# Five tiles in the old form and two pairs, or three tiles and three pairs

## The chip, the cores and the metric

The kernel runs on one core of one Trainium2 chip. The metric is the device time of one execution in microseconds (us); the kernel before takes 1206.51 us, the median of 3 runs (1205.77 to 1207.02). TensorE is called PE, its weight loads PEld, VectorE DVE, ScalarE ACT, GpSimd POOL and SyncE, which issues all DMAs here, SP.

## The reference

Two stages follow one another. The first is a linear attention over 8 batches of 8 heads, 576 positions of width 64, with 128 random features; the second is a gated feed-forward over the 4608 resulting rows of width 512, with a hidden width of 1536. All is float32.

```python
q_p, k_p = phi(q * scale), phi(k * scale)    # phi(x) = exp(h - max h) / sqrt(m), h = x @ omega.T - |x|^2 / 2
kv = einsum('bhsm,bhsd->bhmd', k_p, v);  z = sum(k_p, axis=2)
attn = einsum('bhsm,bhmd->bhsd', q_p, kv) / (einsum('bhsm,bhm->bhs', q_p, z) + 1e-6)
x = attn.transpose(0, 2, 1, 3).reshape(4608, 512)
g = x @ w_gate;  val = x @ w_val             # 512 x 1536 each
out = (g * sigmoid(g) * val) @ w_out         # 1536 x 512
```

## The kernel before, in words

**Attention.** Its work is cut into groups of 256 rows of a pair of heads, 72 groups of q and 72 of k, two groups to a step, so 72 steps (`steps`, `NS`). A loop over n runs the pieces of several steps side by side: transposes of the inputs (`st_transpose`, tile pt, four transposes a step), the projections on omega (`st_project`, tile pp, 16 matmuls a step), the maximum on DVE (`st_max`), eight exponentials on ACT (`st_exp`, tile ph), the sums over k (`k_accumulate`, tile kvacc), and, one to three steps later, q's part (`q_transpose`, `q_mult`, `q_norm`, `q_out`; tiles ptq, po, xt). For batches 0 to 3 `q_mult` works on PE (po), from batch 4 on the normalisation runs on POOL and DVE instead (jk, dj). `q_out` gives columns of x, transposed.

**Feed-forward, old form.** The 4608 rows are 9 tiles of 512. The hidden width is 12 pieces of 128 (f), in 4 sets of 3. A *visit* is one tile with one set: 3 x 12 matmuls for the gate (tile g), 3 x 12 for the value (tile v, both line 657), and 4 x 9 for the way down (tile o, line 666). Every float32 product is three products of a high and a low part (names ending in hi/hh/xh and lo/hl/xl), so the weights and x are split first. The visits go round by round (`ROUNDS`): for every set, all tiles of the round. Before a set's first visit the weights of the next set are fetched from a scratch in DRAM (tile wraw) and split by ACT and POOL (`load_weights`, whi and wlo).

**Feed-forward, new form.** The last tiles go in pairs (`PAIRS`). Two tiles and two pieces of the hidden width make 2 x 2 blocks; seven block products (`ORDER`, line 872, tiles a, c, d, six matmuls each) take the place of eight. `make_seven` forms the seven combinations of the weights on DVE (line 848 and the three after it), `first_x` and `next_x` form those of x on DVE (line 827 in `next_x`), `plus`, `gate` and `value` add the products up on DVE and ACT. The way down stays as it was. One pair has 12 x 42 = 504 products and 288 matmuls of the way down. `next_x` for the following pair starts in a pair's second visit: four DMAs (line 823) and eight subtractions.

**Order of the work.** The first `EARLY` = 25 steps (order `CLOSE`) hold no feed-forward. From then on (order `GROUPED`) every step has six places (`SHARE`) at which `give` takes matmuls from the generator `stream` until the amount that `course` sets for that step is reached. `course` spreads all visits but the last 45 us (`MARGIN`) evenly over the steps to the end, kept below what is available by then. That gave 5.43 us of visits in steps 25 to 33 and 9.40 us from step 34 on, in the planner's own costs. What is left after the last step, 45 us by the same costs, runs while `first_x` prepares the first pair; then the pairs follow.

**Conversion of the weights.** All 36 weight blocks are loaded raw (tiles st), turned into float32 numbers by six operations each (`convert_all`: lines 268 and 276 on ACT, 270, 272 and 274 on DVE, 278 on POOL) and written to the scratch. `tick` issues one operation; `marks` paces them so that a set is ready when its first visit is near. In the profile seven of them end in the first 128.4 us, 12 in the next 97.6 us and 17 in the 264 us after that; the last were due at step 50 (`DENSE`).

```python
for k_ in range(1, NSET):
    at = int(np.searchsorted(course, cum[len(ROUNDS[0]) * k_ - 1]))
    marks.append((max(at, marks[-1][0] + 1), 3 * FA * (k_ + 1)))
DENSE = marks[-1][0]
```

Of the kernel before, what the change touches and what calls it, by code (L numbers as in the profile page):

```python
# [23 lines left out]
def kernel(  # L24
# [34 lines left out]

    ROUNDS = [range(0, 3), range(3, 5)]
    PAIRS = [(5, 6), (7, 8)]
    NPF = NF // 2
    MARGIN = 45.0

# [99 lines left out]
    visits = []  # L166
    for r, tiles in enumerate(ROUNDS):
        sets = list(range(NSET))[:: 1 if r % 2 == 0 else -1]
# [41 lines left out]
# [3 lines that stand above are left out]
# [458 lines left out]
    acc = {}  # L671
    paired = [j for pair in PAIRS for j in pair]

# [117 lines left out]
    def first_x():  # L791

        win = late_pools["win"]
        for c in range(CH):
            x = {}
            for name, j, o in (("b11", 0, 0), ("b21", 0, CH), ("t1", 1, 0), ("b22", 1, CH), ("t3", None, None)):
                x[name] = win.tile([P, T], F32, name=f"first_{name}{c}", tag="first", bufs=5)
                if j is not None:
                    nc.sync.dma_start(x[name], x_dram[PAIRS[0][j]][:, c + o, :])
            yield  # L800
# [18 lines left out]
    def next_x(r):  # L819

        for half, names in ((0, ("b11", "t1")), (1, ("b21", "b22"))):
            for j, name in zip(PAIRS[r], names):
                nc.sync.dma_start(ahead[name], x_dram[j][:, half * CH : (half + 1) * CH, :])
        yield
        for o, a, b in (("t3", "b22", "t1"), ("t1", "t1", "b11"), ("t2", "b22", "t1"), ("t4", "b21", "t2")):
            for c in range(CH):
                nc.vector.tensor_tensor(ahead[o][:, c], ahead[a][:, c], ahead[b][:, c], op=ALU.subtract)
                yield
# [38 lines left out]
    def product(ps, n, wts, start):  # L867
# [10 lines left out]
    pair_visits = [  # L878
        (r, k_, pf) for r in range(len(PAIRS)) for k_, pf in enumerate(list(range(NPF))[:: 1 if r % 2 == 0 else -1])
    ]  # L880

    def pair_rounds(todo):
# [51 lines left out]
        for vi, (r, k_, pf) in enumerate(pair_visits):  # L934
            unit = [0]
            then = pair_visits[vi + 1] if vi + 1 < len(pair_visits) else None
            new_x = then and then[0] != r
            if k_ == 1 and r + 1 < len(PAIRS):
                prep = next_x(r + 1)
# [57 lines left out]
            wts2 = {f: weights[f, 2] for f in (2 * pf, 2 * pf + 1)}  # L997
            for j, o in ((PAIRS[r][1], 1), (PAIRS[r][0], 0)):
                ht = {2 * pf + n: h[2 * n + o] for n in range(2)}
# [124 lines left out]
```

## Time and profile before

| | |
|---|---|
| time, median of 3 runs | 1206.51 us |
| profiled execution, its own time | 1207.78 us |
| its span on the core | 1206.0 us |
| PE busy | 1165.7 us (97%) |
| ACT, DVE, POOL busy | 679.9, 595.7, 572.7 us |
| ACT table loads (exponential and Silu in turn) | 28 and 29, 1283 ns each |
| matmuls of lines 657, 666, 872 | 1440, 1104, 1008 |

A busy share is the union of an engine's instructions; the ends of matmuls are modelled, so a busy PE may still be waiting a little. Times in the views are us from the start of the span. In the tables by window each engine has its busy time and, as (x...), its instructions in the window.

### The profile page before, as it was taken

To read this page: it belongs to the slowest core of one execution; us is meant where nothing else is said; L and a number is where in the kernel's file an instruction comes from. 1 tells how busy PE (TensorE), PEld (TensorE's weight loads), DVE (VectorE), ACT (ScalarE), POOL (GpSimd) and SP (SyncE) were. 2 spreads that over 40 slices of the span, in tenths; PEclk is the share of its full clock that TensorE was granted. 3 is DMA by queue.
4 is the path that set the end of the run, shared out by engine and by line. 5 is a ranking of instruction groups with operands and counts; after the bars stand their busy time and mean duration, and the time that the engine had idled before them with its cause. 6 is when DMAs were issued, how large, how long until landed. Compare 5 with 4: busy or idle time off the path is not lost.

```text
span 1206.0 us, 18814 instructions
## 1 busy us (share of the span) xinstructions
PE 1165.7 (97%) x6705; PEld 964.4 (80%) x6705; DVE 595.7 (49%) x1159; ACT 679.9 (56%) x1497; POOL 572.7 (47%) x500
## 2 busy tenths in 40 slices
PE   6999999999999999999999999999899999999998
PEld 5888787877887778888888787878688888888886
DVE  3687674345454644434332353373534556535544
ACT  4888977576566555556465656343454435454431
POOL 3333343334254546535445776344655543555541
PEclk9999999999999999999999999999999999999999
DMA  6555665344344423345222221334311111321103
GB/s 150 141 136 142 164 201 159 87 125 134 103 118 131 138 74 79 79 107 122 62 60 68 71 66 45 106 87 139 88 53 53 53 44 27 105 53 53 53 18 70
DMA packets 174110, 113.53 MB, mean 94 GB/s; under 512 B 125856, under 2 KB 144320, under 8 KB 174016
## 3 DMA queue, kind: packets, MB, share of 16 engines
q1 hardware_dynamic: 174016, 112.32, 34.9%
q8 instruction: 53, 0.87, 0.3%
q14 instruction: 41, 0.34, 0.1%
HBM read 87.10 MB, written 25.18 MB: 93 GB/s over the span
## 4 chain that ended last, share of the span: by engine, by line
PE 66%; DMA 4%; DVE 3%; POOL 3%; ACT 3%; issue 2%; SPq 1%; POOLq 0%; ACTq 0%; DVEq 0%
PE o L666 22%; PE a L872 10%; PE v L657 8%; PE g L657 8%; PE c L872 5%; PE pp L406 3%; PE d L872 2%; PE kvacc L540 2%; PE ptq L564 2%; PE xt L621 1%; PE pt L383 1%; POOL wlo L251 1%; DMA st<-in_moe_w_out_dram 1%; ACT ph L438 1%; DMA nat<-in_k_dram 1%
## 5 line engine op out<-in xcount | busy, mean ns | idle before, releaser
L438 ACT ACTIVATE ph<-pp,st 128x128 f32<-128x128 f32 x576 | 157.6, 389 | 17.0 <-DVE st L427 16.4
L695 DVE TENSOR_TENSOR acc<-o,acc 128x512 f32<-128x512 f32 x140 | 95.7, 685 | 104.7 <-PE o L666 104.7
L390 POOL TENSOR_TENSOR sq<-nat 128x512 f32<-128x512 f32 x72 | 75.6, 1051 | 146.0 <-DMA nat<-in_k_dram 116.9
L424 DVE TENSOR_REDUCE st<-pp 128x4 f32<-128x512 f32 x144 | 92.8, 683 | 72.5 <-PE pp L406 72.3
L251 POOL TENSOR_TENSOR wlo<-wraw,whi 128x512 fp32r<-128x512 f32 x76 | 99.9, 1324 | 55.3 <-ACT whi L250 55.1
L666 PE MATMUL o<-whi,hh 128*128 128x512 f32 x240 | 97.3, 406 | 3.1 <-ACT sl L731 3.0
L666 PE MATMUL o<-whi,hl 128*128 128x512 f32 x240 | 95.1, 396 | 1.2 <-POOL hl L754 1.2
L657 PE MATMUL g<-xh,whi 128*128 128x512 f32 x240 | 96.1, 400 | 0.0
L657 PE MATMUL v<-xh,whi 128*128 128x512 f32 x240 | 95.7, 399 | 0.2 <-DVE acc L695 0.2
L500 POOL TENSOR_TENSOR jk<-ph,zt 128x512 f32<-128x512 f32 x32 | 41.6, 1305 | 112.8 <-ACT ph L438 112.8
L666 PE MATMUL o<-wlo,hh 128*128 128x512 f32 x240 | 95.1, 396 | 0.0
L406 PE MATMUL pp<-omT,x 64*128 64x128 f32 x1152 | 92.8, 297 | 2.3 <-ACT x L391 2.2
L657 PE MATMUL g<-xh,wlo 128*128 128x512 f32 x240 | 94.0, 392 | 0.0
L657 PE MATMUL v<-xh,wlo 128*128 128x512 f32 x240 | 93.8, 391 | 0.0
L657 PE MATMUL g<-xl,whi 128*128 128x512 f32 x240 | 93.8, 391 | 0.0
L657 PE MATMUL v<-xl,whi 128*128 128x512 f32 x240 | 93.6, 390 | 0.0
L754 POOL TENSOR_TENSOR hl<-sl,hh 128x512 fp32r<-128x512 f32 x60 | 79.0, 1320 | 27.1 <-ACT hh L753 26.9
L406 PEld LDWEIGHTS pp<-omT,x 64*128 64x128 f32 x1152 | 76.0, 196 | 19.1 <-issue 11.6
L417 DVE TENSOR_REDUCE st<-sq 128x8 f32<-128x512 f32 x72 | 49.1, 681 | 85.5 <-POOL sq L390 85.4
L863 POOL TENSOR_TENSOR wlo<-s,whi 128x512 fp32r<-128x512 f32 x44 | 65.3, 1502 | 34.3 <-DVE late L969 11.8
L863 POOL TENSOR_TENSOR wlo<-wraw,whi 128x256 fp32r<-128x256 f32 (+1 forms) x44 | 45.2, 1026 | 74.9 <-ACT whi L862 74.7
L540 PE MATMUL kvacc<-v,ph 128*128 128x65 f32 x512 | 69.3, 277 | 3.4 <-ACT ph L438 3.4
(251 smaller groups left out, 2854.8 us busy)
## 6 DMA issues: line engine op xcount, KB each, us to landing
wraw<-wscr SPq DMA_DIRECT2D x120, 256.0 KB, 2.7
wscr<-wc SPq DMA_DIRECT2D x36, 256.0 KB, 2.4
out_dram<-acc SPq DMA_DIRECT2D x72, 128.0 KB, 2.3
nat<-in_k_dram SPq DMA_DIRECT2D x64, 128.0 KB, 3.1
v<-in_v_dram SPq DMA_DIRECT2D x64, 128.0 KB, 3.2
nat<-in_q_dram SPq DMA_DIRECT2D x64, 128.0 KB, 3.0
st<-in_moe_w_gate_dram SPq DMA_DIRECT2D x12, 512.0 KB, 5.2
st<-in_moe_w_val_dram SPq DMA_DIRECT2D x12, 512.0 KB, 4.6
```

The source lines that it names most:

```text
L251: nc.gpsimd.tensor_tensor(lo, raw, hi.bitcast(F32), op=ALU.subtract)
L390: nc.gpsimd.tensor_tensor(sq, nat, nat, op=ALU.mult)
L406: nc.tensor.matmul(pp[hh][:, i, c, :], x[r, i, c * P : (c + 1) * P], omT[r], start=True, stop=True)
L424: nc.vector.tensor_reduce(st[:, 1, :, :, hh], pp[hh], axis=AX.X, op=ALU.max, negate=True)
L438: nc.scalar.activation(ph[:, c, hh * M : (hh + 1) * M], pp[hh][:, i, c, :], AF.Exp, bias=st[:, 3, i, c, hh : hh + 1], scale=1.0,)
L540: nc.tensor.matmul(acc[:, 2 * (pr % 2) + hh, :], ph[:, c, hh * M : (hh + 1) * M], vt[:, 2 * c + j if gr is None else c, hh, :], start=firs ...
L657: nc.tensor.matmul(ps, a_[:, ws], b_[:, c, :], start=n == 0, stop=n == 3 * NC - 1)
L666: nc.tensor.matmul(ps, a_[:, ts_], b_, start=first and n == 0, stop=last and n == 2)
L695: nc.vector.tensor_tensor(a_, po, a_, op=ALU.add)
L754: nc.gpsimd.tensor_tensor(hl, h, hh.bitcast(F32), op=ALU.subtract)
L863: nc.gpsimd.tensor_tensor(lo, src_, hi.bitcast(F32), op=ALU.subtract)
L872: nc.tensor.matmul(ps, a_[:, w_], b_[:, c, :], start=start and c == 0 and m == 0, stop=c == CH - 1 and m == 2, skip_group_check=True,)
```

## The change

Tiles 3 and 4 leave the old form and become a third pair, worked before the other two. The one round that is left has three tiles.

```diff
-    ROUNDS = [range(0, 3), range(3, 5)]
-    PAIRS = [(5, 6), (7, 8)]
+    ROUNDS = [range(0, 3)]
+    PAIRS = [(3, 4), (5, 6), (7, 8)]
```

Everything else follows from these two tables. There are 12 visits where there were 20, and 18 visits of pairs where there were 12. `course` now gives every step from 25 on 4.87 us of visits. The set changes inside the attention fall from six to three, and the last conversions are due at step 66 instead of 50: from step 36 on 3.6 operations of conversion a step, where there were 6.75 until step 50. The fetch of tiles 3 and 4 as whole tiles (`fetch_x`) is gone, and `next_x` is run twice.

By engine: line 657 has 864 matmuls (1440 before), line 872 has 1512 (1008 before), line 666 as many as before; ACT's table loads in the attention are 20 and 21 (28 and 29 before).

PE, between the transposes of two steps, at step 47 (batch 4; o, g and v are feed-forward, the rest attention). Before:

```order
L383 MATMUL pt_4653<-ident,nat_4311 128x128 x4
L657 MATMUL g_6_4668<-xh_1234,whi_0_3977 128x512
...
L657 MATMUL g_8_4704<-xh_1234,wlo_0_3990 128x512
L666 MATMUL o_2_0_4724<-whi_2_4525,hh_6_4560 128x512
...
L621 MATMUL xt_2_4743<-qt_2_4626,kvr_1_3744 64x256 x2
L406 MATMUL pp_47_4749<-omT,x_4658 128x128
...
L564 MATMUL ptq_3_4759<-ident,ph_45_4486 128x128 x4
L540 MATMUL kvacc_1_4476<-v_102,ph_45_4491 128x65 x4
L383 MATMUL pt_4791<-ident,nat_4437 128x128 x4
```

The same step now:

```order
L383 MATMUL pt_4181<-ident,nat_3922 128x128 x4
L666 MATMUL o_1_3_4193<-whi_2_3655,hh_3_3760 128x512
...
L657 MATMUL v_3_4206<-xh_1234,whi_1_3196 128x512
...
L621 MATMUL xt_2_4226<-qt_2_4154,kvr_1_3487 64x256 x2
L406 MATMUL pp_47_4232<-omT,x_4186 128x128
...
L564 MATMUL ptq_3_4242<-ident,ph_45_4055 128x128 x4
L540 MATMUL kvacc_1_4045<-v_102,ph_45_4060 128x65 x4
L383 MATMUL pt_4274<-ident,nat_4006 128x128 x4
```

Between the transposes and the next projections stood three gates and one row of the way down, 45 matmuls; now one row of the way down and one value, 21. From step 36 on a step holds 33 to 51 such matmuls before and 12 to 28 now; seven steps have 12.

SP, where x of the following pair is loaded (late is x, wraw are weights, out_dram is the output). In the first pair, now, the last of the four loads stands behind two loads of weights that wait for POOL, as it did before:

```order
L306 DMA wraw_0_7798<-wscr 128x512
L306 DMA wraw_0_7800<-wscr 128x512
L823 DMA late_7475<-xs_122 128x1024
L306 DMA wraw_1_7922<-wscr 128x512
L306 DMA wraw_1_7924<-wscr 128x512
```

In the second pair, now, for the third:

```order
L306 DMA wraw_1_9111<-wscr 128x512
L823 DMA late_7474<-xs_123 128x1024
L823 DMA late_7474<-xs_124 128x1024
L823 DMA late_7475<-xs_124 128x1024
L823 DMA late_7476<-xs_123 128x1024
L699 DMA out_dram<-acc_0_7751 64x512
L699 DMA out_dram<-acc_0_7751 64x512
L306 DMA wraw_1_9113<-wscr 128x512
```

Here all four loads stand together, one load of weights ahead of where the first rows of the pair before go out.

DVE, at the same two places in the changed kernel (line 969 adds the products up, 827 forms the next pair's x from late, 848 begins `make_seven`, 839 splits x, 695 adds up the way down). In the first pair:

```order
L851 TENSOR_TENSOR s_0_0_7847<-wraw_0_7798,s_0_0_7847 128x256
L827 TENSOR_TENSOR late_7476<-late_7475,late_7474 128x512 x2
L827 TENSOR_TENSOR late_7474<-late_7474 128x512 x2
L969 TENSOR_TENSOR sl0k<-c_0_7703,late_7478 128x512
L827 TENSOR_TENSOR late_7475<-late_7475,late_7474 128x512 x2
L827 TENSOR_TENSOR late_7477<-late_7476,late_7475 128x512 x2
L969 TENSOR_TENSOR sl2k<-a_0_7702,late_7478 128x512
L969 TENSOR_TENSOR late_7477<-d_0_7704,late_7478 128x512
```

In the second pair:

```order
L839 TENSOR_TENSOR t4lo<-late_7477,t4hi 128x1024
L695 TENSOR_TENSOR acc_3_7963<-o_4_3_8919,acc_3_7963 128x512
L827 TENSOR_TENSOR late_7476<-late_7475,late_7474 128x512
L695 TENSOR_TENSOR acc_0_7751<-o_5_0_8944,acc_0_7751 128x512
L827 TENSOR_TENSOR late_7476<-late_7475,late_7474 128x512
L827 TENSOR_TENSOR late_7474<-late_7474 128x512 x2
L969 TENSOR_TENSOR sl0k<-c_0_8928,late_7478 128x512
L827 TENSOR_TENSOR late_7475<-late_7475,late_7474 128x512
L695 TENSOR_TENSOR acc_1_7780<-o_5_1_8969,acc_1_7780 128x512
```

In both the subtractions of line 827, whose inputs come by those loads, stand ahead of additions that empty products from PSUM. In the first pair they follow the combinations of weights for the next visit; in the second they stand in the first half of the pair's first visit, among the last rows of the pair before.

## The prediction

> **What bounds the kernel now.** I read the page first, then the chain that ended last, then windows over the stages.
>
> ```profile
> span 1206.0 us, 18814 instructions
> PE 1165.7 (97%) x6705; PEld 964.4 (80%) x6705; DVE 595.7 (49%) x1159; ACT 679.9 (56%) x1497; POOL 572.7 (47%) x500
> PE 66%; DMA 4%; DVE 3%; POOL 3%; ACT 3%; issue 2%; SPq 1%; POOLq 0%; ACTq 0%; DVEq 0%
> ```
>
> PE is the bound; no other engine is busy for more than 56%. But 97% mixes stages, so the same table by stage: up to the first visit, attention with visits, the 45 us left over, the pairs (PE, PEld, DVE, ACT, POOL, then clock and DMA).
>
> ```profile
> 0.00:128.40 128.40, 114.20 (x998) 102.93 (x998) 84.45 (x213) 94.31 (x282) 46.76 (x61) 1.00 0.59 147
> 128.40:770.00 641.60, 625.04 (x3851) 511.11 (x3850) 288.36 (x602) 394.70 (x881) 306.58 (x268) 0.99 0.38 102
> 770.00:825.25 55.25, 55.05 (x241) 44.78 (x242) 30.80 (x45) 22.81 (x42) 25.91 (x21) 1.00 0.42 118
> 825.25:1203.00 377.75, 371.42 (x1621) 305.52 (x1619) 192.12 (x300) 168.12 (x295) 193.49 (x153) 0.99 0.22 59
> ```
>
> The change leaves the first stage alone, shortens the second and lengthens the last. In the pairs PE runs without a gap for long stretches; this row of the chain gives the price of a matmul:
>
> ```profile
> 881.29 1.36 PE c L872 x6
> ```
>
> 1.36 / 6 = 0.2267 us. 1621 matmuls at that price are 367.5 of the last stage's 377.75 us; the 10.2 us over lie at its start (below).
>
> **Work that goes and comes.** Eight visits go: 8 x (72 + 36) = 864 matmuls. A pair comes: 504 products and 288 of the way down, 792. The difference, 72 matmuls, is 16.3 us of PE, and since PE is the bound in both stages I count all of it: -16.3. It holds only if each stage's other time, what PE loses beside these matmuls, stays as it is.
>
> **What a thinner attention costs.** Three stretches with whole steps, cut at the copies of x (line 391): a thin one (steps 28 to 34, 5.43 us of visits a step by the planner), a thick one with conversions and set changes (35 to 50), a thick one without conversions (54 to 69). One table for line 657 and one for 666 (PE, then PEld), one for 391 (one a step) and one for 278 (one a converted block):
>
> ```profile
> 154.45:225.85 71.40, 24.26 (x97) 17.36 (x96) 1.00 0.51 144
> 225.95:458.35 232.40, 111.66 (x468) 86.09 (x466) 0.99 0.42 118
> 497.75:713.25 215.50, 109.39 (x467) 86.57 (x466) 1.00 0.33 82
> ...
> 154.45:225.85 71.40, 18.37 (x72) 13.00 (x72) 1.00 0.51 144
> 225.95:458.35 232.40, 51.33 (x199) 38.85 (x200) 0.99 0.42 118
> 497.75:713.25 215.50, 51.71 (x216) 40.03 (x216) 1.00 0.33 82
> ...
> 154.45:225.85 71.40, 4.16 (x7) 1.00 0.51 144
> 225.95:458.35 232.40, 9.36 (x16) 0.99 0.42 118
> 497.75:713.25 215.50, 9.44 (x16) 1.00 0.33 82
> ...
> 154.45:225.85 71.40, 8.34 (x8) 1.00 0.51 144
> 225.95:458.35 232.40, 18.15 (x17) 0.99 0.42 118
> ```
>
> Take from each stretch its visits' matmuls at 0.2267 us and divide by the steps. Thin: 71.4 - 169 x 0.2267 = 33.1, over 7 steps 4.73 us. Thick with conversions: 232.4 - 667 x 0.2267 = 81.2, over 16 steps 5.07. Without: 215.5 - 683 x 0.2267 = 60.7, over 16 steps 3.79. The attention's own PE work in a step from batch 4 on is read from one step, start to start:
>
> ```profile
> 613.14 0.69 PE L621 MATMUL xt<-qt,kvr 128*64 128x64 f32 x16
> 613.75 1.16 PE L406 MATMUL pp<-omT,x 64*128 64x128 f32 x16
> 614.85 0.66 PE L564 MATMUL ptq<-ident,ph 128*128 128x128 f32 x4
> 615.34 1.00 PE L540 MATMUL kvacc<-v,ph 128*128 128x65 f32 x8
> 616.18 0.61 PE L383 MATMUL pt<-ident,nat 128*128 128x128 f32 x4
> 616.54 0.48 PE L657 MATMUL g<-xh,whi 128*128 128x512 f32 x1
> ...
> 307.74 1.00 PE L581 MATMUL po<-kvr,qt 128*128 128x65 f32 x8
> 308.55 0.48 PE L666 MATMUL o<-whi,hh 128*128 128x512 f32 x1
> ...
> 312.76 0.38 PE L614 MATMUL xt<-ident,xn 128*128 128x128 f32 x2
> 313.07 1.16 PE L406 MATMUL pp<-omT,x 64*128 64x128 f32 x16
> ```
>
> 616.54 - 613.14 = 3.40 us. Up to batch 3 there is po (0.81) and a shorter xt (0.31 for 0.61): 3.92. So PE loses 0.81 us a step in the thin stretch, 1.41 in the thick one with conversions (half its steps of either sort, 3.66), 0.39 in the one without. One such loss in full, on ACT and then PE:
>
> ```profile
> 299.50 0.66 ACT L268 ACTIVATE wc<-st 128x512 f32<-128x512 f32 x1 [4.21 <-DMA st<-in_moe_w_out_dram]
> 301.10 0.37 ACT L636 COPY xo<-xt 128x256 f32<-128x256 f32 x1
> 301.53 0.66 PE L383 MATMUL pt<-ident,nat 128*128 128x128 f32 x4 [1.65 <-ACT xo L636]
> ```
>
> ACT stood 4.21 us before a conversion whose raw weights had not landed; the copy of xo behind it came late, and PE waited 1.65 us for its place in PSUM.
>
> From step 35 on there are 41 steps. Before, 16 x 1.41 + 25 x 0.39 = 32.3 us are lost. Now 31 of them (35 to 65) carry the same 17 or 18 conversions and the same three set changes, at about half the density per step, and 10 carry none. Bounds: if conversions and set changes cost what they cost in the thin stretch ((0.81 - 0.39) x 7 / 8 = 0.37 us a block), 18 x 0.37 + 41 x 0.39 = 22.7, a gain of 9.6. If every step with a conversion loses 1.41 and every later one 0.81, 31 x 1.41 + 10 x 0.81 = 51.8, a loss of 19.5. If the cost goes by the block as in the thick stretch, 18 blocks for 17, it is the same within 1 us. I take +4: near that case, since the thin stretch, with as many blocks a step as the thick one, loses less and not more, but above it for the seven steps that hold only 12 matmuls. There PE, from the projections' end to the next projections, has 0.49 + 0.84 + 0.36 + 12 x 0.2267 + 0.61 = 5.0 us to do, and the work that must be done by then is this:
>
> ```profile
> 614.94 1.29 DVE L424 TENSOR_REDUCE st<-pp 128x4 f32<-128x512 f32 x2 [3.66 <-PE pp L406]
> 616.47 0.17 DVE L427 SCALAR_TENSOR_TENSOR st<-st 128x8 f32<-128x8 f32 x1
> 617.41 1.28 ACT L438 ACT_TABLE_LOAD   x1
> 618.71 2.18 ACT L438 ACTIVATE ph<-pp,st 128x128 f32<-128x128 f32 x8
> ```
>
> 1.8 us on DVE, 2.18 on ACT, and 1.28 more where the table was Silu's: 4.0 or 5.3 us, so there is no slack for anything queued on ACT ahead of it.
>
> **What the extra pair costs besides its matmuls.** The 10.2 us at the start of the pairs have one main place, here on DVE, then PE's clock by windows:
>
> ```profile
> 861.51 1.27 DVE L848 TENSOR_TENSOR s<-wraw 128x256 f32<-128x256 f32 x1 [5.26 <-DMA wraw<-wscr]
> 866.24 0.68 DVE L969 TENSOR_TENSOR sl0k<-c,late 128x512 f32<-128x512 f32 x1
> ...
> 869.98 0.79 PE L872 MATMUL a<-t4hi,whi 128*128 128x512 f32 x1 [3.20 <-DVE sl2k L969]
> ...
> 868.90:875.70 6.80, 5.72 (x14) 4.46 (x15) 3.67 (x7) 3.62 (x8) 4.77 (x4) 0.53 0.28 69
> ```
>
> DVE waited for weights, then did subtractions of `next_x`, and only then emptied the products; PE waited 3.20 us and then ran 6.8 us at 0.53 of its clock, which costs 6.8 x 0.47 = 3.2 more. That place stays. `next_x` now runs a second time. The subtractions again stand ahead of the additions, but their loads are issued well ahead and other work lies between. Bounds: nothing, if the loads have landed; 6.4 us and a little, say 8, if it goes as in the first pair. I take +3, under the middle.
>
> The Trainium skill, "TensorE: Matmul & The Clock Gate", section "Why this matters for your kernels", allows "No PE-idle gaps >~3µs between matmul bursts"; after such a gap PE drops to half clock. The trace agrees: 0.53 stands right behind the wait of 3.20 us. By that rule each wait of 3 us that the thinner steps bring would cost some 1.7 us more for 3.4 us at half clock, an estimate from that page; three of them, one a set change, would lift the first rival below by 5 us.
>
> **Sum.** -16.3 + 4 + 3 = -9.3. The profiled execution took 1207.78 us, 1.78 more than its span, and 1.27 more than the median; on the median the sum gives 1206.5 - 9.3 = 1197.
>
> **Rivals.** *Slower: the thin attention waits at every step.* Chains that 9.4 us of visits hid need hiding by 4.87. For it speaks the 1.41 us of the stretch with conversions and the 5.3 against 5.0 us above; against it the thin stretch with 0.81. Price +19.5: 1206.5 - 16.3 + 19.5 + 3 = 1213. It decides from (32.3 + 16.3 - 3) / 41 = 1.11 us lost a step.
>
> *The attention gets cheaper still.* Three set changes, the fetch of tiles 3 and 4 and 16 table loads of 1.28 us leave it; the rest costs as in the thin stretch: 1206.5 - 16.3 - 9.6 + 1 = 1182. Against it: the thin stretch held no set change with its splits of weights.
>
> *The second pair stalls like the first.* 1206.5 - 16.3 + 4 + 8 = 1202. For it speaks that DVE takes its work in order and stands before loads there too; against it the early issue.
>
> **Chances.** Forecast 0.47, slower rival 0.23, cheaper attention 0.14, second stall 0.16. Faster or slower by 0.2% is about what a measurement here can tell from no change, so the bounds are 1204.1 and 1208.9. The forecast and the cheaper attention are faster (0.61), of the second stall 0.10 is; 0.04 of it and 0.06 of the slower rival fall between; 0.02 and 0.17 are slower. Faster 0.71, same 0.10, slower 0.19. The range 1182 to 1213 reaches from the one rival to the other.
>
> **What would show it.** In the new profile the first product should start 196 us less the change in losses earlier, near 825 - 196 + 4 = 633 us, and the pairs should last 378 + 179.5 + 3 = 560 us. Steps 35 to 65 should lose about 1 us each over their matmuls and 3.4 or 3.9. Waits of PE for exp or x copies (pp), missing before, would show the slower rival; waits of DVE line 827 on loads and half clock early in the second pair the stall. I am wrong if the first product starts after 645 us or if PE has gaps of microseconds within the second or third pair.

## The result, and the profile after

The changed kernel takes 1214.71 us (median of 5 runs, 1212.94 to 1219.41); the kernel before, timed beside it, 1205.77. The ratio is 1.0085, with a 95% interval of 1.0057 to 1.0114. It is slower by some 10 us; 1197 was forecast.

Three rows of the new page (span, busy times, and the group of the exponentials with its idle time and what ended it):

```profile
span 1217.3 us, 18970 instructions
PE 1162.8 (96%) x6633; PEld 961.6 (79%) x6633; DVE 668.3 (55%) x1266; ACT 688.7 (57%) x1539; POOL 593.0 (49%) x515
L438 ACT ACTIVATE ph<-pp,st 128x128 f32<-128x128 f32 x576 | 157.3, 389 | 43.8 <-DVE st L427 43.5
```

The last of them in the kernel before:

```profile
L438 ACT ACTIVATE ph<-pp,st 128x128 f32<-128x128 f32 x576 | 157.6, 389 | 17.0 <-DVE st L427 16.4
```

PE has 72 matmuls less, and yet the span has grown by 11.3 us. ACT's idle time before the exps, nearly all of it ended by VectorE's last operation on the maximum, is 43.8 us (17.0 before). The new table by stage says where this shows (columns as in the prediction):

```profile
0.00:128.40 128.40, 114.76 (x1016) 102.79 (x1017) 87.29 (x217) 96.14 (x289) 48.76 (x63) 1.00 0.61 150
128.40:600.00 471.60, 441.45 (x2942) 359.73 (x2941) 257.88 (x549) 315.38 (x767) 236.68 (x212) 0.96 0.41 113
600.00:655.37 55.37, 55.37 (x266) 45.02 (x265) 30.20 (x45) 23.20 (x42) 18.69 (x16) 1.00 0.44 124
655.37:1214.00 558.63, 551.19 (x2413) 454.02 (x2411) 292.95 (x455) 253.94 (x444) 288.86 (x227) 0.99 0.22 62
```

The first product starts at 655.37 us, 169.9 earlier than before (825.25). 864 matmuls at 0.2267 us are 195.9, so the attention lost 26.0 us more than it did. From the first product to the end of the span it is 561.9 us instead of 380.75, 181.2 more, where 792 matmuls make 179.5: 1.7 lost. -16.3 + 26.0 + 1.7 = 11.4, the growth of the span (11.3) but for rounding. These are two single executions, and that of the changed kernel (1219.41 us) is the slowest of its five; by the medians, 8.9 us apart, the attention lost 8.9 + 16.3 - 1.7 = 23.5 us more. In the attention PE's gaps are 30.1 us (471.60 - 441.45; 16.6 before, in a stretch a third longer) and the mean clock is 0.96 instead of 0.99.

PE's waits by line and releaser, the longest (us in total, times, longest):

```profile
PE pp L406 <- ACT ph L438: 8.3, 6, 4.0
PE pt L383 <- ACT xo L636: 8.1, 5, 3.6
PE pt_om L319 <- DMA om<-in_omega_dram: 5.0, 1, 5.0
PE zp L460 <- ACT kvr L454: 4.3, 1, 4.3
PE xt L621 <- ACT x L391: 4.1, 1, 4.1
PE a L872 <- DVE sl2k L969: 3.2, 1, 3.2
```

The first, which the kernel before does not have, is PE waiting for its projections' place in PSUM until the exps of the step before have read it. The third stands ahead of all steps, in the kernel before too (5.2 us). One of the first's six waits, on PE, ACT, DVE and POOL in turn; each engine works in order:

```profile
410.66 0.65 PE L621 MATMUL xt<-qt,kvr 128*64 128x256 f32 x4
415.34 2.59 PE L406 MATMUL pp<-omT,x 64*128 64x128 f32 x16 [4.02 <-ACT ph L438]
...
413.63 2.17 ACT L438 ACTIVATE ph<-pp,st 128x128 f32<-128x128 f32 x8 [3.50 <-DVE st L427]
...
408.42 0.92 DVE L272 TENSOR_SCALAR wc<-wc 128x512 int32<-128x512 int32 x1
409.37 1.67 DVE L274 SCALAR_TENSOR_TENSOR st<-st,wc 128x512 int32<-128x512 int32 x1
410.96 1.27 DVE L424 TENSOR_REDUCE st<-pp 128x4 f32<-128x512 f32 x2
412.27 1.13 DVE L426 SCALAR_TENSOR_TENSOR st<-st 128x8 f32<-128x8 f32 x1
413.43 0.17 DVE L427 SCALAR_TENSOR_TENSOR st<-st 128x8 f32<-128x8 f32 x1
...
409.01 1.48 POOL L251 TENSOR_TENSOR wlo<-wraw,whi 128x512 fp32r<-128x512 f32 x1
411.12 1.04 POOL L278 TENSOR_TENSOR wc<-st 128x512 int32<-128x512 int32 x1 [0.63 <-DVE st L274]
412.11 1.26 POOL L754 TENSOR_TENSOR hl<-sl,hh 128x512 fp32r<-128x512 f32 x1
```

DVE was busy with conversions ahead of the maximum, and two of its operations are far over their usual length (medians of 0.69 and 0.17 us): L274 takes 1.67 us and ends at 411.04, behind POOL's subtraction (409.01 + 1.48 = 410.49); L426, on 8 numbers a partition, takes 1.13 and ends at 413.40, POOL's L754 at 413.37. So VectorE looks held by GpSimd; no run tests this alone. The maximum came late, so the exps, so PE. Another, on DVE and POOL:

```profile
552.52 1.28 POOL L251 TENSOR_TENSOR wlo<-wraw,whi 128x512 fp32r<-128x512 f32 x1
553.76 1.27 POOL L754 TENSOR_TENSOR hl<-sl,hh 128x512 fp32r<-128x512 f32 x1
554.99 2.04 POOL L516 TENSOR_TENSOR ph<-ph,dj 128x512 f32<-128x512 f32 x2
556.99 1.04 POOL L390 TENSOR_TENSOR sq<-nat 128x512 f32<-128x512 f32 x1
...
558.06 0.69 DVE L417 TENSOR_REDUCE st<-sq 128x8 f32<-128x512 f32 x1 [3.43 <-POOL sq L390]
```

Here POOL had a queue, with a split of a weight block (wlo) in it; the squares sq came late, DVE waited 3.43 us for them, and 5 us later PE waited 4.13 for a copy behind the exps. What such a wait costs beyond itself shows in the clock, around the first of the two (PE, PEld, DVE, ACT, POOL, clock and DMA):

```profile
404.00:415.34 11.34, 6.27 (x47) 4.79 (x43) 9.46 (x13) 6.01 (x16) 8.85 (x8) 1.00 0.55 173
415.34:425.50 10.16, 10.13 (x47) 9.13 (x48) 3.25 (x8) 8.15 (x20) 3.53 (x4) 0.52 0.48 121
425.50:435.50 10.00, 10.00 (x64) 8.03 (x64) 3.33 (x8) 5.45 (x9) 2.59 (x3) 0.98 0.24 58
```

PE waits 4.02 us and then runs 10.2 us at 0.52 of its clock. The trace's clock records give 34.1 us of half clock before the pairs, in six pieces of 3.41, 6.83 or 10.24 us; before it were two pieces, 6.8 us. Half of the difference, 13.6 of the 26 us, is time lost to the slow clock; the other 12 are about what PE's gaps grew by (30.1 less 16.6).

### The profile page after: what moved, and what is told of

It is laid out like the page before. It is cut to its first block, busy times and chain, and to the rows that moved or that the text cites. A ratio compares the mean times of both kernels' runs of the same rounds, so it can differ in the third digit from the quotient of the medians.

```text
span 1217.3 us, 18970 instructions
## 1 busy us (share of the span) xinstructions
PE 1162.8 (96%) x6633; PEld 961.6 (79%) x6633; DVE 668.3 (55%) x1266; ACT 688.7 (57%) x1539; POOL 593.0 (49%) x515
## 5 line engine op out<-in xcount | busy, mean ns | idle before, releaser
L438 ACT ACTIVATE ph<-pp,st 128x128 f32<-128x128 f32 x576 | 157.3, 389 | 43.8 <-DVE st L427 43.5
L390 POOL TENSOR_TENSOR sq<-nat 128x512 f32<-128x512 f32 x72 | 76.1, 1057 | 121.5 <-DMA nat<-in_k_dram 87.8
L863 POOL TENSOR_TENSOR wlo<-wraw,whi 128x512 fp32r<-128x512 f32 (+1 forms) x64 | 66.6, 1041 | 116.8 <-ACT whi L862 116.4
L863 POOL TENSOR_TENSOR wlo<-s,whi 128x512 fp32r<-128x512 f32 x64 | 95.8, 1513 | 49.9 <-DVE late L969 18.7
L251 POOL TENSOR_TENSOR wlo<-wraw,whi 128x512 fp32r<-128x512 f32 x59 | 77.0, 1309 | 42.0 <-ACT whi L250 41.9
L417 DVE TENSOR_REDUCE st<-sq 128x8 f32<-128x512 f32 x72 | 49.0, 681 | 72.7 <-POOL sq L390 67.8
L666 PE MATMUL o<-whi,late 128*128 128x512 f32 x192 | 74.5, 389 | 0.0
L965 ACT COPY late<-a 128x512 f32<-128x512 f32 x72 | 42.0, 584 | 51.1 <-PE a L872 48.3
L862 ACT CAST whi<-wraw 128x512 fp32r<-128x512 f32 (+1 forms) x64 | 32.9, 514 | 66.7 <-PE a L872 48.2
L540 PEld LDWEIGHTS kvacc<-v,ph 128*128 128x128 f32 x512 | 66.5, 201 | 4.1 <-ACT ph L438 3.7
L278 POOL TENSOR_TENSOR wc<-st 128x512 int32<-128x512 int32 x36 | 37.7, 1048 | 58.7 <-DVE st L274 12.2
L657 PE MATMUL g<-xh,whi 128*128 128x512 f32 x144 | 61.0, 424 | 0.0
L754 POOL TENSOR_TENSOR hl<-sl,hh 128x512 fp32r<-128x512 f32 x36 | 47.7, 1327 | 24.6 <-ACT hh L753 22.8
L383 PE MATMUL pt<-ident,nat 128*128 128x128 f32 x288 | 49.5, 294 | 10.4 <-ACT xo L636 8.1
```

Source lines behind the costliest of these rows:

```text
L251: nc.gpsimd.tensor_tensor(lo, raw, hi.bitcast(F32), op=ALU.subtract)
L383: nc.tensor.transpose(pt[:, i, c * P : (c + 1) * P], nat[:, i, c].rearrange("p h d -> p (h d)"), ident)
L390: nc.gpsimd.tensor_tensor(sq, nat, nat, op=ALU.mult)
L438: nc.scalar.activation(ph[:, c, hh * M : (hh + 1) * M], pp[hh][:, i, c, :], AF.Exp, bias=st[:, 3, i, c, hh : hh + 1], scale=1.0,)
L540: nc.tensor.matmul(acc[:, 2 * (pr % 2) + hh, :], ph[:, c, hh * M : (hh + 1) * M], vt[:, 2 * c + j if gr is None else c, hh, :], start=firs ...
L657: nc.tensor.matmul(ps, a_[:, ws], b_[:, c, :], start=n == 0, stop=n == 3 * NC - 1)
```

## The experiments

At the start there were three theories. A: the conversions of the weights, which the thinner visits have to cover for longer. B: the thin visits by themselves. C: what else the change moved (which tiles and sets are worked when). A2 is A with the splits of the weight blocks added.

**The kernel before, thinned: e1 and e8.** More of the planner's visits are left for behind the last step. The conversions, which `marks` paces by the visits, spread with them: the last are due at step 66 in e1, as in the changed kernel.

```diff
-    MARGIN = 45.0
+    MARGIN = 240.552    # e1: 4.87 us of visits a step, as in the changed kernel
+    MARGIN = 140.0      # e8: 7.14 us a step from step 34 on
```

> The kernel before with the margin raised from 45 to 240.55 us: tiles, pairs and matmuls as before, but every step of the attention from 25 on holds 4.87 us of visits as in the changed kernel, and the eight visits of tiles 3 and 4 run after the attention. In the traces of before and after, the attention with its visits lost 26.0 us more after the change than before (825.25 - 655.37 = 169.9 us shorter where 864 matmuls at 0.2267 are 195.9). Theory A (the thin attention lets what stands ahead in ACT's and DVE's queues reach PE, and half clock follows each long wait) and theory B (a thin step is too short by itself, whatever stands in the queues): about 26 us slower than before, 1226 to 1234. Theory C (it is not density but the other order of sets and tiles in the single round): within 5 us of before, 1201 to 1211.

> The kernel before with the margin at 140 us: 349 us of visits in 51 steps, 6.84 us a step, between the 4.87 of the thin run (25 to 28 us slower) and the 8.7 of the kernel before. If the loss falls evenly with the density, 11 to 14 us slower than before, 1215 to 1219. If it sets in only where a step is about as long as the chain (near 8.3 us of PE work), 0 to 5 us slower, 1203 to 1209.

e1 (2 runs): 1231.17 us, 1.0242 of the kernel before (1.0163 to 1.0321), its first product at 850.66, 25.4 us later than before, the pairs as they were. e8: 1217.19, 1.0109 (1.0051 to 1.0166), first product at 836.4, 11.2 later. e8 takes 95 us of visits out of the 42 steps from step 34 on, 2.26 us each, which leaves 7.14; the 6.84 of its expectation is the mean over all 51. At 9.40, 7.14 and 4.87 us a step (the planner's amounts) the attention loses 0, 11 and 25 us more, nearly even steps. So thinning, with the slower conversions that come with it, costs about what the change lost; C falls.

**Without the conversions: e2 and e3.** The five operations of lines 268 to 276 are left out of either kernel; the sixth, one operation on POOL, stays.

```diff
-            nc.scalar.activation(u, r, AF.Abs)              # and lines 270, 272, 274, 276
-            nc.gpsimd.tensor_tensor(ui, ri, low, op=ALU.add)
+            nc.gpsimd.tensor_tensor(u, r, r, op=ALU.mult)
```

> The changed kernel without the conversion of the weights: lines 268, 270, 272, 274 and 276 are left out, each block is squared by one operation of POOL of the same size in place of the last step, and loads, stores to the scratch, splits and all matmuls stay; so the weights and the output are other numbers. Theory A, with the conversions as the main thing in the queues: the losses of the attention fall from 58 us to some 20, so about 1175, and 10 to 16 us under the kernel before without conversions. Theory B: the losses stay at 45 or more, 1200 or above, and above the kernel before without conversions.

> The kernel before with the same left out. It lost 32 us from step 35 on by my count, 16 of them in the 16 steps with conversions. Theory A: about 16 to 20 us under before, 1186 to 1190, and 10 to 16 above the changed kernel without conversions. Theory B: the same time for this one, but below the changed kernel without conversions.

The changed kernel takes 1193.29 (0.9894; 0.9852 to 0.9936), the kernel before 1191.86 (0.9894; 0.9868 to 0.9921): level, where A had the changed one well below and B above; e2 lies between the times that the two gave for it. In the profiled executions the first products are at 633.09 and 805.89, 172.8 us apart, so 23.1 of the 195.9 are still lost. By the medians, 1.4 us apart where the matmuls and the pairs give -14.6, 16 are lost instead of 23.5. A profiled execution is one sample (e2's is 3.5 us over its median, e3's 5.2 under), and its half clock varies (e2 has 34 us of it before the pairs, e3 14), so I rest nothing on the 23. A in its strong form falls.

**The conversions in the first three places of a step only: e4 and e14.** Then they are done before the maximum and the exps come.

```diff
-                for _ in range(int(np.ceil((want - ticks[0]) / left))):
+                slots_ = left if n < EARLY else max(left - 3, 1)
+                for _ in range(int(np.ceil((want - ticks[0]) / slots_))):
```

> The changed kernel with the operations of the conversion issued in the first three of a step's six places only, right behind the exponentials, in place of all six, so that DVE has them behind it when the next maximum comes. Same operations, same pace per step. Theory A says DVE's part of the delay (exponentials waited 31.6 us on the maximum, 4.6 before) shrinks: 5 to 12 us under the changed kernel, 1203 to 1210. Theory B: no difference, 1211 to 1218.

> The kernel before with its conversions in the first three of each step's six places only, as was done to the changed kernel, which came out 2 us better by it. If the late places are what the conversions cost, this one gains 2 to 4 us as well: 1200 to 1204 with the kernel before at 1204 to 1206, a version that beats both. If that was chance, it is level with the kernel before, within 0.2%.

The changed kernel took 1212.40 (1.0064; 1.0030 to 1.0099), 2 us less, which the intervals do not tell from nothing. The kernel before became slower, which neither case of its expectation had: 1210.83 (1.0054; 1.0021 to 1.0087). The place of the conversions is no lever.

**Without conversions and splits: e5 and e11.** As e2 and e3, and the blocks that replace an old set go from the scratch straight into their high part, which serves as the low part too.

```diff
-        fetched = fetch((f,), i)
         new_weights(f, i)
-        split_piece(f, i, fetched[0])
+        hi, _ = weights[f, i]
+        nc.sync.dma_start(hi.bitcast(F32), wscr[f, i])
+        weights[f, i] = hi, hi
```

> The changed kernel with, beside the arithmetic of the conversion, the splits of the weights at the three set changes left out: the block is loaded from the scratch straight into the high part, and the matmuls take the high part where they took the low one, so matmuls, loads and stores are as many as before the edit; ACT's and POOL's lumps of three splits are gone, and the output is other numbers. Without the conversions alone the attention with its visits took 633.1 us (first product), 23 us more than the kernel before without conversions would leave. Theory A2 (lumps of splits stand in POOL's and ACT's queues ahead of what a thin step needs at once): first product near 610 us, no wait of PE over 2.5 us, time 1170 to 1178. Theory B (a thin step is too short by itself): first product 628 to 634, time 1188 to 1194.

> The kernel before without the conversions of the weights and without their splits (both left out: the blocks come from the scratch as they are, and the low part is the high part), the control to the changed kernel with the same left out, whose first product was at 625.0 and whose time was 1188.8. Theory B (thin visits cost by themselves, whatever the work beside them): the 195.9 us of matmuls still give back only 172 to 178, so the first product is at 797 to 803 and the time 1177 to 1184, five to twelve below the changed kernel's. Theory A2 (all the work on the weights is what thin visits don't cover): without it the visits give back 190 to 196, first product 815 to 821, time 1194 to 1200, five or more above the changed kernel's.

1188.82 (0.9851; 0.9774 to 0.9927) and 1188.73 (0.9913; 0.9883 to 0.9943), from 2 and 4 runs on two chips, so that the ratios are to be compared and not the times. First products at 624.99 and 810.7: 185.7 apart, 10.2 lost. e5's product lies between what the two theories gave for it, nearer B's 628 to 634, and e11's lies between as well: part of the loss is this work. With all of it gone the change is no longer slower.

**The splits spread out, and the places spread out: e6 and e7.** e6 issues each split behind the matmuls of its own block instead of three at a time. e7 spreads the six places for visits over the step.

```diff
-            if new_set:                                     # e6, behind the gates of a visit
-                for f in fs:
-                    load_weights(nxt[1] * FA + f - fs[0], 0)
+                if new_set:                                 # e6, behind each gate
+                    load_weights(nxt[1] * FA + f - fs[0], 0)
...
         q_out,                                              # e7, in GROUPED
+        SHARE,
         st_project,
         q_transpose,
+        SHARE,
...
         st_max,
+        SHARE,
         st_exp,
...
         SHARE,
-        SHARE,
-        SHARE,
         lambda n: q_norm(n + 1),
...
         SHARE,
-        SHARE,
         SHARE,
```

> The changed kernel complete, with the splits of a set change spread: the three gate blocks are loaded and split each behind its own gate's matmuls and not all three behind the last, and the three blocks of the way down one behind each value of the following visit. Theory A2: a third to a half of the 26 us comes back, 1200 to 1207. Theory B: 1210 to 1217.

> The changed kernel complete, with the six places for visits moved apart: one behind the columns of x, one behind the transposes of q, one behind the maxima, three as before behind the transposes of the inputs. Two or three blocks of visits a step now lie between different waits, so PE has work in front of the wait for the copy of xo and of the sums over k, and the copies have longer. The chain from the projections over maximum and exponential to the next projections is as long as before. Waits for xo, kvr and x were 8.1 + 2.5, 4.3 and 4.1 us, with half clock behind the long ones. Theory A and A2: 8 to 15 us faster than the changed kernel, 1200 to 1207. Theory B, with the chain over the exponentials as the limit: less than 4 us, 1211 to 1215.

Neither gained. e6 took 1217.23 (1.0093; 1.0057 to 1.0130), where B had it. e7 (2 runs) took 1238.48 (1.0262; 1.0159 to 1.0366), slower than both theories had it. Its largest waits of PE:

```profile
PE xt L621 <- ACT x L391: 20.4, 10, 4.5
PE xt L614 <- ACT x L391: 7.3, 5, 3.0
```

The next step's transposes (pt) and the outputs (xt) share one tile of PSUM. The visits had stood between them; moved away, they uncover the copy of x that frees the tile.

**A tile of PSUM of its own for xt: e9 and e10.**

```diff
-            po = (ps_att if n + OLAG < EARLY or i else ps_tr)(f"xt{b}_{g}", [P, G])
+            po = ps_moe(f"xt{b}_{g}", [P, G])
```

> The changed kernel with the transposed outputs xt of every step (line 609) put into the visits' PSUM tiles (three of them in rotation) instead of the single tile that the transposes of the next step's q and k use, or the single one of the q products. Theory S (the single tiles: PE waits since a tile is to be copied out before the next thing may be written into it): PE's waits pt <- ACT xo (8.1 us in the changed kernel) and xt <- ACT x (4.1) fall below 2 together, the half clock behind them too, so the first product of the pairs comes at 645 to 650 instead of 655.4, time 1203 to 1209. Theory Q (the queues of ScalarE and VectorE are late there, whatever tile it is): the waits come back at another line (xt for a visit's tile, pp for the exps), first product 653 to 658, time 1211 to 1216.

> The kernel before with the same edit, as the control. Theory S: its own waits on these tiles (xo 5.7, xn 5.2) are of the same size but with less half clock behind them: 1199 to 1204, first product 819 to 822 instead of 825.3. Theory Q: 1204 to 1209. Should this kernel gain as much as the changed one, the single tiles are no reason for the difference between the two.

1220.14 (4 runs; 1.0184; 1.0128 to 1.0241), some 4 us more than Q had, and 1206.43 (1.0026; 0.9998 to 1.0055). The waits at the shared tile went and came back elsewhere, in e9 as these:

```profile
PE pp L406 <- ACT ph L438: 11.9, 6, 3.6
PE pp L406 <- ACT x L391: 7.2, 8, 3.7
PE xt L614 <- DVE xn L591: 6.2, 5, 3.6
```

Theory Q: ScalarE and VectorE are late, whatever tile PE meets them at. The waits on PE name the symptom.

**Without the splits alone: e12 and e13.** The edit of e5, with the conversions kept.

> The changed kernel without the splits of the blocks that replace an old set beside the attention (lines 298 to 300: the block comes from the scratch straight into the high part, and the low part is the high part); the conversions stay. With the conversions left out the two kernels came out level (1193.3 and 1191.9), with both left out too (1188.8 and 1188.7), where the change is 10 us slower with all the work in place. Reading W (any large part of the work on the weights, taken away, lets the thin visits cover the rest): here too the two come out level, within 4 us of each other, both at 1196 to 1204, and this kernel's first product comes at 638 to 648. Reading K (it is the conversions on VectorE and ScalarE that the thin visits don't cover, the splits matter little): this kernel stays 8 to 12 us above the other: 1206 to 1212, first product 648 to 655.

> The kernel before with the same splits left out, on the same chip as the control. Reading W: 1196 to 1204, first product 812 to 822, level with the changed kernel. Reading K: 1196 to 1203, 8 to 12 under the changed kernel.

1195.92 (0.9929; 0.9902 to 0.9957) and 1202.30 (1.0011; 0.9989 to 1.0033), on the same chip. Against 1.0085 for the whole changed kernel the splits are worth 1.6%, some 19 us, in it, and nothing in the kernel before. The edit takes 27 splits out of the changed kernel and 54 out of the kernel before. This is the run that settles most: 54 splits, hidden under 9.4 us of visits a step, cost nothing; 27 of them show under 4.87. First products at 626.73 and 821.27: 194.5 apart, so of 195.9 us only 1.4 are lost instead of 26. But e12's profiled execution (1188.32 us) is 7.6 under its median; by the medians, 6.4 us apart where 14.6 are due, some 8 are still lost, of 23.5. The gains of e2 and e12 overlap: with both gone (e5 and e11, by their ratios) some 7 are lost, give or take 10. What that rest is stays open. K, by which the splits would matter little, is wrong; W has the sense but not the size.

**Which part of a split: e15 to e18.** A split is a transfer, a copy on ACT and a subtraction on POOL. e15 and e16 do the subtraction on VectorE; e17 leaves the splits as they are and does the attention's squares on VectorE; e18 does both. The subtractions moved are the 27 of the set changes beside the attention (54 in e16); the 59 in e15's expectation count 32 in the pairs too, which stay on GpSimd. Nothing is left out of these kernels.

```diff
-        split_piece(f, i, fetched[0])                                # e15, e16, e18
+        split_piece(f, i, fetched[0], nc.vector)   # the engine of line 251's subtraction
...
-        nc.gpsimd.tensor_tensor(sq, nat, nat, op=ALU.mult)           # e17, e18
+        nc.vector.tensor_tensor(sq, nat, nat, op=ALU.mult)
```

> The changed kernel with the subtraction of the low parts of the blocks that replace an old set (line 251 as called from line 300: 59 blocks of 1.31 us) on VectorE instead of GpSimd; the copy of the high part on ScalarE stays. Theory G (GpSimd's queue: the subtractions lie ahead of the squares and the products that the attention's own chain waits for, DVE st <- POOL sq 51.2 us and dj <- POOL jk 57.0 in the stretch from 128 to 600 us): most of what came back without any split comes back here, first product 632 to 643, time 1197 to 1206, level with the kernel before or under it. Theory D (the block's way in: its wait for the transfer and ScalarE's copy, or VectorE that has no room either): first product 652 to 665, time 1212 to 1224.

> The kernel before with the same edit. Both theories: there the splits cost nothing that shows (without them 1202.3 beside 1202.1), so level with the kernel before within 0.4%; VectorE queued behind ScalarE's copy can make it slower by some us.

> The changed kernel with the squares of the next step's q and k (line 390: 72 of 1.06 us) on VectorE instead of GpSimd, so that VectorE's sum of them and the maximum no longer wait for GpSimd's queue (51.2 us in the stretch from 128 to 600 us). Theory G: the exps come earlier, the waits pp <- ACT ph (8.3) go, first product 638 to 650, time 1199 to 1211. Theory D: VectorE's 72 x 0.68 us more only make it later: first product 655 to 670, time 1215 to 1228.

> The changed kernel with both moved to VectorE: the subtractions of the low parts of the replaced blocks (line 251 from line 300) and the squares (line 390). Each alone took the changed kernel from 1.0085 of the kernel before to 0.9965 and 0.9991. Theory G with two separate causes (the gains add, GpSimd's queue is then short for the products of q too): 1188 to 1196, first product 628 to 636. Theory G with one cause (either edit empties the queue enough, and VectorE, then 75% busy beside the attention, is the next to be late): 1196 to 1206, first product 638 to 646.

| | time, median | ratio to the kernel before | profiled execution: time, first product |
|---|---|---|---|
| changed kernel | 1214.71 | 1.0085 (1.0057 to 1.0114) | 1219.41, 655.4 |
| e15, subtraction on VectorE | 1198.66 | 0.9965 (0.9934 to 0.9996) | 1205.10, 642.1 |
| e17, squares on VectorE | 1201.37 | 0.9991 (0.9964 to 1.0018) | 1205.30, 641.4 |
| e18, both | 1188.97 | 0.9855 (0.9826 to 0.9884) | 1188.27, 625.1 |
| e16, subtraction, in the kernel before | 1200.91 | 0.9995 (0.9968 to 1.0022) | 1194.67, 813.8 |

The last of these executions is the fastest of its eleven, without any half clock before the pairs, so its early first product is not put down to the edit; the medians show no gain.

Theory G is the one that came: the transfer and ScalarE's copy are still there, and 1.2 of the 1.6% that the splits cost come back. The two gains add (1.2 and 0.9%, together 2.3%; e18's first product is 3 us earlier than even the case with two causes had it), and e18 is 1.45% under the kernel before and some 2.3% under the changed one, the version that beats both. Its stages:

```profile
128.40:575.00 446.60, 431.92 (x2957) 353.46 (x2958) 296.85 (x621) 314.77 (x763) 164.18 (x143) 0.99 0.43 119
575.00:625.13 50.13, 50.13 (x239) 41.23 (x237) 29.07 (x43) 21.41 (x38) 15.55 (x13) 1.00 0.43 123
625.13:1183.50 558.37, 550.18 (x2413) 453.14 (x2411) 291.89 (x455) 253.97 (x444) 289.28 (x227) 1.00 0.22 62
```

DVE has taken on work (296.85 us in the 446.60, 66%; 55% in the changed kernel's 471.60), POOL is down from 236.68 us to 164.18, PE's gaps from 30.1 us to 14.7, and the clock is back at 0.99. VectorE's groups from 128 to 600 us: the sum over the squares (L417) and the small operations on the denominators (L505) in the changed kernel, with POOL's group of the subtraction (L251); then the same in e18, where L251 and the squares (L390) are VectorE's; last the sum in the kernel before:

```profile
L417 DVE TENSOR_REDUCE st<-sq 128x8 f32<-128x512 f32 x44 | 30.0, 682 | 56.0 <-POOL sq L390 51.2 <-ACT acc L692 4.8
L505 DVE TENSOR_SCALAR dj<-dj 128x4 f32<-128x4 f32 x36 | 14.4, 400 | 0.7
...
L251 POOL TENSOR_TENSOR wlo<-wraw,whi 128x512 fp32r<-128x512 f32 x27 | 35.1, 1306 | 18.1 <-ACT whi L250 18.1
```

```profile
L390 DVE TENSOR_TENSOR sq<-nat 128x512 f32<-128x512 f32 x43 | 39.1, 909 | 27.3 <-DMA nat<-in_k_dram 23.0 <-DMA nat<-in_q_dram 4.2
L417 DVE TENSOR_REDUCE st<-sq 128x8 f32<-128x512 f32 x44 | 29.9, 680 | 0.7
L251 DVE TENSOR_TENSOR wlo<-wraw,whi 128x512 fp32r<-128x512 f32 x27 | 22.6, 857 | 5.4 <-ACT whi L250 5.3
L505 DVE TENSOR_SCALAR dj<-dj 128x4 f32<-128x4 f32 x36 | 8.7, 241 | 0.6
```

```profile
L417 DVE TENSOR_REDUCE st<-sq 128x8 f32<-128x512 f32 x38 | 26.0, 684 | 65.5 <-POOL sq L390 65.5
```

The wait of 51.2 us for the squares is gone, though VectorE itself now waits 27.3 us for the loads of nat, and the same 36 operations on four numbers a partition take 241 ns instead of 400. Neither figure measures the loss: the kernel before, the faster of the two, waits 65.5 us for the squares, and e12, 19 us faster than the changed kernel, still has 44.3 us and 384 ns. ACT's idle time before the exps tells the two edits apart: 43.8 us in the changed kernel, 44.2 in e15, 27.5 in e17 and 28.3 in e18 (17.0 before). Moving the squares brings the exps forward (PE's waits for them fall from 8.3 to 5.5 us in e17, and do not go as was expected). Moving the subtractions does not; its gain shows in PE's other waits behind ACT (for xo 3.7 us instead of 8.1, for x of xt 2.1 instead of 4.1, for kvr 1.6 instead of 4.3) and in 17.1 us of half clock before the pairs instead of 34.1. That POOL's queue delays the chain and that POOL's work holds VectorE up would both give this; no run takes one away and keeps the other, so their shares stay open. So does how the kernel before would do with both edits: only the subtraction was moved there, and that came out level.

## Why the prediction was wrong

- **-16.3 for the matmuls: right.** The counts are as given, and so is the price: 792 matmuls more in the pairs are 179.5 us by it, and 181.2 were measured.
- **+3 for the second `next_x`: nearly right.** The whole of the pairs lost 1.7 us. The second pair's first visit has two short waits, not for VectorE's subtractions, and no half clock behind them; it is the lower bound that came true:

```profile
861.43 0.50 PE L872 MATMUL c<-b22hi,whi 128*128 128x512 f32 x1 [0.58 <-ACT late L965]
876.58 0.50 PE L872 MATMUL a<-t2hi,whi 128*128 128x512 f32 x1 [1.26 <-ACT late L965]
```

- **The stall at the start of the pairs stays: right** (3.18 us now, 3.20 before, and half clock behind it).
- **+4 for the thin attention: this step failed. It was +26** by the traces and 23.5 by the medians, beyond its own upper bound of 19.5 either way. By the working of the prediction on the new trace, steps 35 to 65 (line 657, then 666; PE):

```profile
222.65:527.65 305.00, 118.05 (x468) 0.97 0.43 117
...
222.65:527.65 305.00, 49.39 (x199) 0.97 0.43 117
```

  305.0 - 667 x 0.2267 = 153.8 us, over 31 steps 4.96. With 8 steps of 3.92 and 23 of 3.40 the attention's own work is 109.6, and 44.2 are lost, 1.43 a step. That is near the 1.41 of the upper bound, but by chance: the mean hides two sorts of steps. The same stretch cut at step 43 (PE, PEld, DVE, ACT, POOL, clock and DMA):

```profile
222.65:298.15 75.50, 74.55 (x530) 63.26 (x529) 35.19 (x79) 58.48 (x138) 28.41 (x25) 1.00 0.47 125
298.15:527.65 229.50, 210.66 (x1390) 169.77 (x1389) 132.35 (x264) 145.29 (x355) 129.01 (x116) 0.96 0.42 115
```

  The first 8 steps hold 176 matmuls of visits and lose 0.53 each by the same working, less than the thin stretch before; the other 23 hold 493 and lose 1.72. PE's gaps are 0.95 us in the first row and 18.8 in the second. From there on q's normalisation is on POOL (its first product jk starts at 307.0 us), which is busy for 38% of the first row and 56% of the second. The next five steps (54.85 us with 124 matmuls), without conversions, lose 1.95 each, where the upper bound had 0.81. So the loss came with the thin steps from batch 4 on, and not evenly by the step or by the converted block; no run moves the normalisation alone, so its part in it is not shown. All 36 steps lose 54 us, by themselves 22 more than the 32.3 of all steps from 35 on before.
- **Why the estimate was low.** I took the cost from the thin stretch of the old trace, steps 28 to 34, which lost only 0.81 a step. That stretch held no set change, and so no split; the prediction said so, but held it against the cheaper rival alone and not against the +4. It also lay wholly before q's normalisation moved to POOL (349.1 us in that trace), a difference between the batches that the prediction counted for PE only. And I treated what a stretch loses as belonging to the work in it, while e12 and e13 show that splits cost 0 or 19 us by the cover over them.
- **The sentence on slack was the right one.** 5.0 us of PE work against 4.0 to 5.3 us of maximum and exps left "no slack for anything queued on ACT ahead". It moved the +4 only a little and should have led. What was late stood on POOL, and on DVE ahead of the maximum, further back than I looked.
- **The slower rival, 1213, was the case that came**, with waits of pp for the exps as its sign, the one named. That its 1213 lies so near is partly luck: its price, 19.5, was some 4 us short by the medians, mainly in the later steps (1.95 each where it had 0.81), and its +3 was 1.3 too much. The Trainium skill's page "TensorE: Matmul & The Clock Gate", section "Why this matters for your kernels", was named there, with 5 us for three waits of 3 us; the trace agrees on the kind (0.52 behind 4.02 us), though not on the limit of some 3 us (half clock stood behind waits of 1.1 to 1.7 us too, see the last section), and has 34.1 us of half clock in the attention, 13.6 us more lost than before, in six pieces where before it had two, three of them of 6.8 or 10.2 us.

## What to carry to other kernels

When work is taken off the engine that bounds a stage, ask first what it was covering: per step, compare what that engine still has to do between a result and its next use with the whole chain back to it, through every in-order queue on the way, and not only the last engine. A cost read under thick cover, or under thin cover without the work in question, says little of that work under thin cover; here splits worth 0 us became worth 19 with half as many of them. If the chain is then late, look for the engine whose queue holds both filler and the chain (GpSimd here) and move one of them, rather than the place in which PE is seen to wait.

## What the hardware showed

- Some VectorE operations beside a GpSimd instruction take far longer than usual and end shortly behind it: 1.67 us for L274 (median 0.69) and 1.13 for L426 on 128x8 (median 0.17), ending 0.55 and 0.03 us behind one of POOL's. The Trainium skill, "SBUF — State Buffer", section "Who interferes with whom", says that the two share a pair of ports, that some VectorE operations take it, and that the one to come second is blocked for the whole instruction. The trace agrees closely for L426, and roughly for L274. "Perfetto Trace Analysis", section "Optimizing Scalar/DVE Operations", warns for that reason that moving work between the two "might not help"; here moving 27 subtractions and 72 squares from GpSimd to VectorE gave some 2.3% (1214.71 to 1188.97 us).
- Half clock came in pieces of 3.41, 6.83 or 10.24 us, the longest behind one wait of 4.02 us, so that it cost another 5.1 us in this way. It came behind short waits too, where the rule of the Trainium skill named above has gaps over some 3 us. In the changed kernel (PE, then the window behind it):

```profile
179.96 0.61 PE L406 MATMUL pp<-omT,x 64*128 64x128 f32 x2 [1.13 <-ACT ph L438]
...
180.20:187.00 6.80, 6.80 (x30) 5.33 (x30) 3.94 (x9) 5.62 (x9) 1.04 (x1) 0.50 0.45 151
```

  In the kernel before one of the two pieces stands behind the wait of 1.65 us that the prediction shows. Why some pieces are longer than others was not tried.
- The same 27 subtractions take 1306 ns each on GpSimd in the changed kernel and 857 on VectorE in e18, beside GpSimd's other work, so the move also shortens the sum of both.
